# Second half's spectra read into the place of K's second spectrum, with four banks for the last transform and two middle row groups transformed ahead of the mixing

## The chip, the core and the metric

The kernel runs on one core of a Trainium2 chip. The metric is device time in microseconds, the median of several executions of one program. Engines are named as in the profile: PE (TensorE matmuls), PEld (its weight loads), DVE (VectorE), ACT (ScalarE), POOL (GpSimd), SP (SyncE, which here only issues DMAs).

## What is computed

A block of a model with two parts, on 2048 rows of 512 channels, in float32:

```python
h = _layernorm(x, axis=-1) * (1 + ca) + sa
x = x + ga * _A_ref(h, ...)      # long convolution by FFT: K from an SSM, Uf * Kf, inverse FFT
h = _layernorm(x, axis=-1) * (1 + cb) + sb
x = x + gb * _B_ref(h, B_w1, B_w2, B_w3, B_w4)
# _B_ref: gelu(layernorm(h) @ w1), four shifts along the rows, @ w2, + h;
#         then gelu(layernorm(.) @ w3) @ w4
```

## The kernel before, in words

The order of the instructions on every engine is written out by hand. It has four stages.

First the convolution kernel K is made and the input is normalised and transformed (until about 245 us of the trace). Then come 16 steps `(jh, kc)`, eight for each half `jh` of the channels: the spectra of the input and of K (tile `VK[jh]`, 32 KB in each partition) are made, multiplied, transformed back one level (`back`), and stored in DRAM as `ZT[jh]`.

The third stage is the last level of the inverse transform, with matmuls against the constant `FI`. `load_inv(jh, k)` reads one eighth of `ZT[jh]`, 512 KB, or 256 KB for half of it. The result is needed by row groups `g` (0 to 3) and halves `i`: 256 rows each, added to the tile `X2` (the trace calls it KX). A group 0 or 3 needs spectra 0, 3, 4 and 7; a group 1 or 2 needs spectra 1, 2, 5 and 6. `inv_half` makes the rows in a bank of PSUM and DVE adds them to X2; `inv_onto` first puts X2 into the bank with an identity matmul, lets the rows accumulate onto it, and ACT copies the sum back. The banks are `py` (pool `psy`, two of them) and `pm` (pool `psw`).

The fourth stage is the MLP part. It works on eight tiles `t` of 256 rows, in the order 7, 0, 1, 2, ...: statistics (`first_stats`), scale and shift (`mix_mod1`, `mix_mod2` on DVE), normalisation (`mix_norm` on ACT, `h<-h,nm,rs`), transposes on PE (`pT`), high and low parts (`parts_of`: ACT `nh`, then DVE `nl`), the product with w1 in two halves (`mix_half`: PE `pm`, 48 matmuls in pairs; ACT `go`), and a store to DRAM (`GD`). The channel part (`chan`, w3 and w4) follows tile by tile. Tiles 7 and 0 need row groups 3 and 0, tiles 1 and 2 come from rows of groups 0 and 1, tile 4 and later from group 2.

So the second half of the channels (`jh` = 1) must be read back right before the mixing starts. Its `ZT[1]` is complete only after the last `back`. Before the change, its eight spectra are read into six blocks `ld`, which also serve other loads: the first four take blocks that are free, the spectra 1 and 5 take the blocks of w2 (free when DVE has split w2), and 2 and 6 take the blocks of 3 and 7 (free when PE has transformed group 3 and group 0). All twelve reads stand on SP's queue, one behind the other. Meanwhile `keep(n)` issues n matmuls whose results are not used.

Rows of group 1 (`a10`, `a11`) are transformed between the two halves of tile 7's product, those of group 2 (`a20`, `a21`) behind the transposes of tiles 0 and 1.

Of the kernel before, what the change touches and what calls it, by code (L numbers as in the profile page):

```python
# [7 lines left out]
F32 = mybir.dt.float32  # L8
# [4 lines left out]
PSUM = bass.MemoryType.PSUM  # L13
# [96 lines left out]
def dram(t, off, ap):  # L110
    return bass.AP(tensor=t.tensor, offset=t.offset + off, ap=ap)


def body(ctx, tc, A):
# [6 lines left out]
    def act(out, in_, f=AF.Copy, scale=1.0, bias=0.0):  # L121
        return S.activation(out, in_, f, bias=bias, scale=scale)  # L122
# [105 lines left out]
    def mod_sum(n):  # L228
        k = MODS[n]
        m = psu.tile([128, 512], F32, name="pu")  # L230
        T.matmul(m, SP4, wmt.pop(n)[:, 0], start=True, stop=True)
        if k in (1, 4):
            return lambda: act(mods[k], m, AF.Identity, bias=1.0)
        return lambda: act(mods[k], m)
# [263 lines left out]
    side = {k: [] for k in range(40)}  # L498
    for k in range(8):
        w, i = ("w3", k) if k < 4 else ("w4", k - 4)  # L500
        n = A[w].shape[0] // 4
# [3 lines left out]
    for n in range(3, 6):  # L505
        k = 7 * n - 9
# [33 lines left out]
    with tc.manual_schedule():  # L540
# [13 lines left out]
        late = [lambda: later.append(mod_sum(2))]  # L554
# [36 lines left out]
        for f in later:  # L591
# [5 lines left out]
    a2 = ExitStack()  # L597
# [4 lines left out]
    VK = [v0x.enter_context(pool("v0", side="right")).tile([128, 64, 2, 64], F32, name="VK0"),  # L602
          c2.tile([128, 64, 2, 64], F32, name="VK1")]
# [6 lines left out]
    block = lambda: ldp.tile([128, 4, 256], F32, name="ld")  # L610
# [18 lines left out]
    vus, zis, zcs = {}, {}, {}  # L629
# [27 lines left out]
    def spectrum_k(jh, kc):  # L657
        p = [kbank([128, 2, 2, 128]) for gh in range(2)]
        for i in range(2):
            for ro in range(2):  # L660
                for ri in range(2):
                    for kk in range(2):
                        for gh in range(2):
                            k1 = kc * 4 + 2 * kk + i
                            rows = slice(gh * 64, gh * 64 + 64)
                            w = T2[k1 // 16][rows, k1 % 16]
                            if ri == gh:
                                w = w[:, ro * 64:ro * 64 + 64]
                            elif ro == ri:
                                w = w[:, gh * 64:gh * 64 + 64]  # L670
                            else:
                                w = T3[rows, k1]
                            T.matmul(p[gh][kk * 64:kk * 64 + 64, i, ro], w,  # L673
                                     VK[jh][rows, ri * 32 + k1].rearrange("p j g -> p (j g)"),
                                     start=(ri == 0), stop=(ri == 1), skip_group_check=True)
        return p
# [32 lines left out]

    def load_inv(jh, k, i=None, q=Y):  # L710
        if (jh, k) not in zis:
            zis[jh, k] = block() if jh or k in (1, 2, 5, 6) else zip_.tile([128, 4, 256], F32, name="zi")
        a, n = (0, 4) if i is None else (2 * i, 2)
        q.dma_start(zis[jh, k][:, a:a + n], dram(ZT[jh], (k * 4 + a) * 32768, [[256, 128], [32768, n], [1, 256]]))

# [3 lines left out]
    def inv_rows(p, jh, g, i, first):  # L719
        for e in range(2):  # L720
            b = g * 4 + i * 2 + e
            for bp, (c, sg) in enumerate(((31 - b, 1), (15 - b, 1), (b, 0), (16 + b, 0))):
                T.matmul(p[bp * 32:bp * 32 + 32, e], FI[:, c, sg], zis[jh, c // 4][:, c % 4],
                         start=first, stop=True, skip_group_check=True)

    def rows_of(jh, g, i):
        return X2[:, g * 4 + i * 2:g * 4 + i * 2 + 2, jh * 256:jh * 256 + 256]

    def inv_half(jh, g, i, pl, name):
        p = pl.tile([128, 2, 256], F32, name=name)  # L730
        inv_rows(p, jh, g, i, True)
        x = rows_of(jh, g, i)
        return lambda: V.tensor_add(x, p, x)

    def inv_onto(jh, g, i, pl, name):
        p = pl.tile([128, 2, 256], F32, name=name)
        x = rows_of(jh, g, i)
        T.matmul(p, ident, x, start=True, stop=False, skip_group_check=True)

        def rows():  # L740
            inv_rows(p, jh, g, i, False)
            return lambda: act(x, p)
        return rows
# [51 lines left out]
    def first_stat(b):  # L795
        if (b + 2) % 16 < 10:
            half_stat(b, 1)
            V.bn_aggr(mv1[:, b], st1[:, (b + 2) % 16])
        else:
            stats(mv1[:, b], X2[:, b])  # L800
        rstd(rs1[:, b:b + 1], mv1[:, b, 1:2])

    def first_stats(g):
        first_stat(2 * g)
        first_stat(2 * g + 1)
# [9 lines left out]
    def parts_of(ps):  # L815
        hi = [cm.tile([128, 2, 256], F32R, name=f"nh{j}") for j in range(2)]
        lo = [cm.tile([128, 2, 256], F32R, name=f"nl{j}") for j in range(2)]
        for j in range(2):
            act(hi[j], ps[j])
            V.tensor_sub(lo[j], ps[j], hi[j].bitcast(F32))  # L820
        return [hi[k // 2][:, k % 2] for k in range(4)], [lo[k // 2][:, k % 2] for k in range(4)]
# [3 lines left out]
    def mix_mod1(g):  # L825
        mh[g] = (cm.tile([128, 2, 512], F32, name="h2"), cm.tile([128, 2, 2], F32, name="mv"),
                 cm.tile([128, 2], F32, name="rs"), cm.tile([128, 2], F32, name="nm"))
        for i in range(2):
            mod1(mh[g][0][:, i], 2 * g + i)

    def mix_mod2(g, i, near=False):
        h, mv, r, nm = mh[g]
        mod2(h[:, i], 2 * g + i)
        stats(mv[:, i], h[:, i])
        if near:
            V.tensor_scalar(r[:, i:i + 1], mv[:, i, 1:2], 1e-5, None, op0=OP.add)
            V.tensor_scalar(nm[:, i:i + 1], mv[:, i, 0:1], -1.0, None, op0=OP.mult)
            P.tensor_tensor(r[:, i:i + 1], r[:, i:i + 1], pw[:, :1], op=OP.pow)
            P.tensor_tensor(nm[:, i:i + 1], nm[:, i:i + 1], r[:, i:i + 1], op=OP.mult)
            return  # L840
        rstd(r[:, i:i + 1], mv[:, i, 1:2])
        P.tensor_tensor(nm[:, i:i + 1], mv[:, i, 0:1], m_one[:, :1], op=OP.mult)
        P.tensor_tensor(nm[:, i:i + 1], nm[:, i:i + 1], r[:, i:i + 1], op=OP.mult)

    def mix_norm(g):
        h, mv, r, nm = mh[g]
        for i in range(2):
            act(h[:, i], h[:, i], AF.Identity, scale=r[:, i:i + 1], bias=nm[:, i:i + 1])
# [98 lines left out]
    def mix_half(t, hl, hf, between=None):  # L947
        p = mix_w(hl, hf, between)
        go = gop.tile([128, 2, 256], F32, name="go")
        act(go, p, AF.Gelu_apprx_tanh)  # L950
        mix_out(t, hf, go)
# [163 lines left out]
    with tc.manual_schedule():  # L1115
# [13 lines left out]
        for n, st in enumerate(steps):  # L1129
            p = spectrum_k(*st)  # L1130
            multiply(*st, us, p)
            if n == 7:
# [4 lines left out]
                zip_ = zix.enter_context(pool("zi", bufs=4, side="right", reuse_waits="tile"))  # L1137
# [12 lines left out]
            if n == 11:  # L1150
                for k in (0, 3, 4, 7):
                    load_inv(0, k)
            if n == 12:
                for k in (1, 2, 5, 6):
                    load_inv(0, k)
# [15 lines left out]
        tp = lambda name, bufs=1, **k: pool(name, bufs, reuse_waits="tile", **k)  # L1171
# [6 lines left out]
            act(W2h[:, i], w2r[i // 2][:, i % 2])  # L1178
        psT = ctx.enter_context(tp("psT", space=PSUM))
        psw = ctx.enter_context(tp("psw", 2, space=PSUM))  # L1180
        psy = a2.enter_context(tp("psy", 2, space=PSUM, side="right"))
        def keep(n):
            d = psT.tile([128, 2, 256], F32, name="pT0").rearrange("p a b -> p (a b)")
            for _ in range(n):
                T.matmul(d, W1h[:, 0, :128], W1h[:, 0], start=True, stop=True)
# [17 lines left out]
        for k in (1, 2):  # L1203
# [1 line left out]
            load_inv(1, k + 4)  # L1205
        onto = [inv_onto(1, g, i, pl, n) for g, i, pl, n in
                ((3, 1, psy, "py"), (0, 0, psy, "py"), (3, 0, psw, "pm"), (0, 1, psw, "pm"))]
        keep(8)
        for f in [f() for f in onto]:
            f()  # L1210
        first_stats(7)
        keep(14)
        mix_mod1(7)
        mix_mod2(7, 0, True)
        mix_mod2(7, 1, True)
        mix_norm(7)
        first_stats(0)
        mix_mod1(0)
        hl = parts_of(transposed(mh.pop(7)[0]))
        mix_mod2(0, 0, True)  # L1220
        mix_mod2(0, 1, True)
        mix_half(7, hl, 0)
        a10 = inv_half(1, 1, 0, psy, "py")
        a11 = inv_half(1, 1, 1, psy, "py")
        mix_norm(0)
        first_stats(1)
        a10()
        mix_half(7, hl, 1)
        mix_mod1(1)
        hl = parts_of(transposed(mh.pop(0)[0]))  # L1230
        mix_mod2(1, 0)
        mix_mod2(1, 1)
        a11()
        a20 = inv_half(1, 2, 0, psy, "py")
        mix_half(0, hl, 0)
        mix_norm(1)
        first_stats(2)
        mix_half(0, hl, 1)
        mix_mod1(2)
        hl = parts_of(transposed(mh.pop(1)[0]))  # L1240
        a21 = inv_half(1, 2, 1, psy, "py")
        mix_mod2(2, 0)
        a20()
        mix_mod2(2, 1)
# [33 lines left out]
        n = cm.tile([128, 2, 512], F32, name="h2")  # L1278
# [49 lines left out]
```

## Time and profile before

| what | value |
|---|---|
| median of 3 executions | 679.2 us (676.43 to 679.76) |
| the profiled execution: its own time | 677.66 us |
| its span in the trace | 675.9 us |
| mean granted TensorE clock | 0.997 |
| busy share of the span: PE, DVE, ACT, POOL | 94%, 73%, 50%, 17% |

The span runs from the first to the last instruction; the execution's own time has 1.76 us more around it. The profiled execution is 1.54 us below the median.

### The profile page before, as it was taken

The page shows a single profiled execution, that of the slowest core. Times are in us where ns is not written, and L with a number is a line of the kernel's source. Part 1 is how long each engine was busy: PE and PEld are TensorE (multiplying, and loading weights), DVE is VectorE, ACT ScalarE, POOL GpSimd, SP SyncE. Part 2 cuts the span into 40 slices and gives each one's busy share as a digit, 9 for nine tenths or more (in the row PEclk, how much of TensorE's full clock was granted, in tenths as well). Part 3 has the DMA queues.
Part 4 walks back from the last instruction along what each step waited for, and adds up shares of the span by engine and source line. Part 5 has one row for each costly group of instructions (what it writes and reads, how often), then busy time and mean ns, then how long its engine had stood idle before and what let it go on. Part 6 is the DMA issues. An engine that isn't in the chain of part 4 may idle for free.

```text
span 675.9 us, 16884 instructions
## 1 busy us (share of the span) xinstructions
PE 636.7 (94%) x7205; PEld 508.2 (75%) x7205; DVE 494.2 (73%) x797; ACT 335.8 (50%) x511; POOL 113.7 (17%) x220
## 2 busy tenths in 40 slices
PE   2899999999999998988999999999999999999996
PEld 1556555665568876645889899898998989898895
DVE  7889999999996897897889777454674445363622
ACT  5778998898884666624456334132141213122121
POOL 2102212112207133203643002010010000000000
PEclk9999999999999999998999999999999999999999
DMA  9602274642838999966386020110100201010001
GB/s 318 277 2 75 75 230 107 197 136 76 294 71 296 302 361 377 366 199 194 118 267 232 1 64 1 55 40 16 57 22 31 64 18 46 1 63 1 1 32 31
DMA packets 49923, 86.43 MB, mean 128 GB/s; under 512 B 4532, under 2 KB 38328, under 8 KB 47256
## 3 DMA queue, kind: packets, MB, share of 16 engines
q1 hardware_dynamic: 44904, 60.97, 28.3%
q0 software_dynamic: 4624, 23.86, 9.8%
q8 instruction: 56, 0.92, 0.6%
q10 hardware_dynamic: 320, 0.52, 0.3%
q14 instruction: 19, 0.16, 0.1%
HBM read 59.12 MB, written 32.90 MB: 136 GB/s over the span
## 4 chain that ended last, share of the span: by engine, by line
PE 72%; DMA 5%; DVE 5%; ACT 3%; issue 2%; POOL 1%; SPq 1%; ACTq 0%; DVEq 0%; POOLq 0%
PE xx L440 7%; PE pm L856 7%; PE pm L854 7%; PE pm L853 7%; PE pa L972 6%; PE pa L973 6%; PE pa L980 6%; PE pk L673 4%; PE kp L490 3%; DMA w4l<-Dw 2%; PE pz L695 2%; PE pk L643 2%; PE ph L911 2%; PE ph L910 2%; PE ph L913 2%
## 5 line engine op out<-in xcount | busy, mean ns | idle before, releaser
L122 ACT ACTIVATE gh<-pm 128x512 fp32r<-128x512 f32 (+1 forms) x48 | 26.9, 561 | 199.2 <-PE pm L856 199.2
L853 PE MATMUL pm<-nh,w3h 128*128 128x256 f32 (+1 forms) x352 | 85.9, 278 | 0.0
L854 PE MATMUL pm<-nh,w3l 128*128 128x256 f32 (+1 forms) x352 | 85.7, 279 | 0.1
L964 DVE TENSOR_TENSOR gl<-gf,gh 128x512 fp32r<-128x512 f32 (+1 forms) x48 | 30.9, 643 | 68.1 <-ACT gf L122 68.1
L972 PE MATMUL pa<-w4h,gh 128*128 128x512 f32 (+1 forms) x176 | 69.6, 395 | 0.0
L973 PE MATMUL pa<-w4l,gh 128*128 128x512 f32 (+1 forms) x176 | 68.9, 392 | 0.0
L854 PEld LDWEIGHTS pm<-nh,w3l 128*128 128x128 f32 (+1 forms) x352 | 65.2, 185 | 2.0 <-DVE w3l L767 0.3
L853 PEld LDWEIGHTS pm<-nh,w3h 128*128 128x128 f32 (+1 forms) x352 | 65.3, 186 | 1.4
L856 PE MATMUL pm<-nl,w3h 128*128 128x256 f32 (+1 forms) x352 | 54.9, 277 | 0.1
L774 POOL TENSOR_TENSOR rs<-mv,eps_t 128x1 f32<-128x1 f32 (+1 forms) x35 | 9.2, 264 | 267.3 <-DVE mv L780 251.5
L980 PE MATMUL pa<-w4h,gl 128*128 128x512 f32 (+1 forms) x176 | 48.0, 390 | 0.0
L441 PE MATMUL xx<-MG,ON 64*128 64x512 f32 x160 | 47.1, 390 | 0.0
L440 PE MATMUL xx<-MG,ON 64*128 64x512 f32 x160 | 47.1, 390 | 0.0
L856 PEld LDWEIGHTS pm<-nl,w3h 128*128 128x128 f32 (+1 forms) x352 | 46.6, 185 | 0.3 <-DVE nl L820 0.3
L916 DVE TENSOR_TENSOR h<-h,ph 128x512 f32<-128x512 f32 x16 | 11.0, 688 | 45.0 <-PE ph L913 45.0
L458 DVE SCALAR_TENSOR_TENSOR e<-tr,p 128x512 f32<-128x512 f32 x64 | 41.1, 684 | 1.7 <-ACT tr L122 1.4
L467 DVE TENSOR_TENSOR e<-tr,p 128x1024 f32<-128x1024 f32 x32 | 39.0, 1218 | 1.1 <-ACT tr L122 1.1
L490 PEld LDWEIGHTS kp<-e,e 128*32 128x32 f32 x2048 | 30.1, 110 | 12.7 <-issue 7.5
L468 DVE TENSOR_TENSOR e<-tr,m 128x1024 f32<-128x1024 f32 x32 | 39.0, 1218 | 0.0
L122 ACT ACTIVATE p<-xx 128x1024 f32<-128x1024 f32 (+1 forms) x40 | 37.5, 980 | 2.1 <-PE xx L258 0.6
L980 PEld LDWEIGHTS pa<-w4h,gl 128*128 128x128 f32 (+1 forms) x176 | 33.0, 188 | 7.1
L673 PE MATMUL pk<-VK,xu 64*64 64x128 f32 x768 | 35.9, 270 | 2.2 <-issue 2.2
(259 smaller groups left out, 1709.8 us busy)
## 6 DMA issues: line engine op xcount, KB each, us to landing
VU<-vs SPq DMA_DIRECT2D x64, 128.0 KB, 3.6
ld<-VU SPq DMA_DIRECT2D x16, 512.0 KB, 7.5
ZT<-z POOLq DMA_DIRECT2D x30, 256.0 KB, 6.3
Dw<-in_w POOLq DMA_DIRECT2D x8, 688.0 KB, 4.6
xu<-in_u SPq DMA_DIRECT2D x4, 1024.0 KB, 8.6
KX<-in_x POOLq DMA_DIRECT2D x4, 1024.0 KB, 9.0
ld<-ZT SPq DMA_DIRECT2D x8, 512.0 KB, 5.6
win<-GD SPq DMA_DIRECT2D x32, 128.0 KB, 2.5
```

The source lines that it names most:

```text
L122: return S.activation(out, in_, f, bias=bias, scale=scale)
L440: T.matmul(x[:, :512], la, ma, start=(i == 0), stop=(i == len(ops) - 1))
L441: T.matmul(x[:, 512:], lb, mb, start=(i == 0), stop=(i == len(ops) - 1))
L458: V.scalar_tensor_tensor(e0[:, 1, a], tr[:, 1, 0], 1.0 - 2.0 * a, mg[:, a], op0=OP.mult, op1=OP.mult)
L490: T.matmul(kp[32 * j:32 * j + 32, (k % 2) * 4 + g], e1[:, r, d], e0[:, r, :, d * 32:d * 32 + 32], start=(r == 0), stop=(r == 1), skip_grou ...
L673: T.matmul(p[gh][kk * 64:kk * 64 + 64, i, ro], w, VK[jh][rows, ri * 32 + k1].rearrange("p j g -> p (j g)"), start=(ri == 0), stop=(ri == 1 ...
L853: T.matmul(p, wh[:, k, c], hi[k], start=(k == 0), stop=False)
L854: T.matmul(p, wl[:, k, c], hi[k], start=False, stop=False)
L856: T.matmul(p, wh[:, k, c], lo[k], start=False, stop=(k == 3))
L972: T.matmul(acc[i], gh[:m, e, s], W4h[:m, f], start=(f == 0), stop=False)
L973: T.matmul(acc[i], gh[:m, e, s], W4l[:m, f], start=False, stop=False)
L980: T.matmul(acc[i], gl[:m, e, s], W4h[:m, f], start=False, stop=(f == 10))
```

## The change

The second half's eight spectra no longer take blocks `ld`: each has a place of 4 KB a partition in `VK[1]`, the tile that held K's second spectrum. `psy` has four banks in place of two. Both halves of group 1 are now made with `inv_onto` (their identity matmuls stand with the other four, their sums are copied by ACT), and both groups 1 and 2 are transformed ahead of tile 7's transposes. The first `keep(8)` is dropped and `keep(14)` becomes `keep(6)`.

```diff
     def load_inv(jh, k, i=None, q=Y):
         if (jh, k) not in zis:
-            zis[jh, k] = block() if jh or k in (1, 2, 5, 6) else zip_.tile([128, 4, 256], F32, name="zi")
+            if jh:
+                zis[jh, k] = VK[1].rearrange("p a b c -> p (a b c)")[:, k * 1024:k * 1024 + 1024].rearrange("p (n d) -> p n d", n=4)
+            else:
+                zis[jh, k] = block() if k in (1, 2, 5, 6) else zip_.tile([128, 4, 256], F32, name="zi")
...
-        psy = a2.enter_context(tp("psy", 2, space=PSUM, side="right"))
+        psy = a2.enter_context(tp("psy", 4, space=PSUM, side="right"))
...
-        keep(8)
+        late = [inv_onto(1, 1, i, psy, "py") for i in range(2)]
         for f in [f() for f in onto]:
             f()
         first_stats(7)
-        keep(14)
+        keep(6)
+        late = [f() for f in late]
+        a20 = inv_half(1, 2, 0, psy, "py")
+        a21 = inv_half(1, 2, 1, psy, "py")
         mix_mod1(7)
         mix_mod2(7, 0, True)
         mix_mod2(7, 1, True)
         mix_norm(7)
+        for f in late:
+            f()
         first_stats(0)
         mix_mod1(0)
         hl = parts_of(transposed(mh.pop(7)[0]))
         mix_mod2(0, 0, True)
         mix_mod2(0, 1, True)
         mix_half(7, hl, 0)
-        a10 = inv_half(1, 1, 0, psy, "py")
-        a11 = inv_half(1, 1, 1, psy, "py")
         mix_norm(0)
         first_stats(1)
-        a10()
         mix_half(7, hl, 1)
         mix_mod1(1)
         hl = parts_of(transposed(mh.pop(0)[0]))
         mix_mod2(1, 0)
         mix_mod2(1, 1)
-        a11()
-        a20 = inv_half(1, 2, 0, psy, "py")
         mix_half(0, hl, 0)
...
         hl = parts_of(transposed(mh.pop(1)[0]))
-        a21 = inv_half(1, 2, 1, psy, "py")
         mix_mod2(2, 0)
         a20()
         mix_mod2(2, 1)
```

PE, from the last rows of the first half's transform to tile 7's product, before (a matmul of this listing appears as two in the trace; `FI` is the transform's constant, `w1h` alone marks `keep`):

```order
L723 MATMUL py<-ld,FI 32x256 x16
L738 MATMUL py<-KX,ident 128x512 x2
L738 MATMUL pm<-KX,ident 128x512 x2
L1185 MATMUL pT_4604<-w1h 128x512 x8
L723 MATMUL py<-ld,FI 32x256 x16
L723 MATMUL pm<-ld,FI 32x256 x16
L1185 MATMUL pT_4657<-w1h 128x512 x14
L812 MATMUL pT_4710<-ident,h_4672 128x128 x4
L812 MATMUL pT_4711<-ident,h_4672 128x128 x4
L853 MATMUL pm<-nh_4720,w1h 128x256
```

The same place of PE after the change (lines of the changed file are three higher):

```order
L726 MATMUL py<-ld,FI 32x256 x16
L741 MATMUL py<-KX,ident 128x512 x2
L741 MATMUL pm<-KX,ident 128x512 x2
L741 MATMUL py<-KX,ident 128x512 x2
L726 MATMUL py<-VK_3051,FI 32x256 x16
L726 MATMUL pm<-VK_3051,FI 32x256 x16
L1188 MATMUL pT_4644<-w1h 128x512 x6
L726 MATMUL py<-VK_3051,FI 32x256 x32
L815 MATMUL pT_4725<-ident,h_4685 128x128 x4
L815 MATMUL pT_4726<-ident,h_4685 128x128 x4
L856 MATMUL pm<-nh_4735,w1h 128x256
```

Thirty-two matmuls of groups 1 and 2 have come in ahead of tile 7's transposes; they stood in three places of the mixing (16, 8 and 8), where nothing stands now.

ACT, from the same stage, before (`KX<-py` and `KX<-pm` are the copies of `inv_onto`, `h` the normalisation, `nh` the high parts of the transposed tile):

```order
L122 ACTIVATE KX<-py 128x2x256 x2
L122 ACTIVATE KX<-pm 128x2x256 x2
L122 ACTIVATE h_4672<-h_4672,nm,rs 128x512 x2
L122 ACTIVATE nh_4720<-pT_4710 128x512
L122 ACTIVATE nh_4721<-pT_4711 128x512
```

And after:

```order
L122 ACTIVATE KX<-py 128x2x256 x2
L122 ACTIVATE KX<-pm 128x2x256 x2
L122 ACTIVATE h_4685<-h_4685,nm,rs 128x512 x2
L122 ACTIVATE KX<-py 128x2x256 x2
L122 ACTIVATE nh_4735<-pT_4725 128x512
L122 ACTIVATE nh_4736<-pT_4726 128x512
```

Two copies (group 1's sums) now stand between the normalisation of tile 7 and its high parts; in their place two adds `KX<-py` are gone from DVE. SP's and POOL's queues issue the same transfers in the same order, SP's twelve reads into another tile.

## Rows read from the trace of the kernel before

**Rows 1.** The page: the span, and each engine's busy time.
```profile
span 675.9 us, 16884 instructions
PE 636.7 (94%) x7205; PEld 508.2 (75%) x7205; DVE 494.2 (73%) x797; ACT 335.8 (50%) x511; POOL 113.7 (17%) x220
```

**Rows 2.** Windows by stage: busy us of each engine, granted clock, DMA share, GB/s.
```profile
300.00:306.00 6.00, 2.26 (x13) 1.47 (x15) 4.10 (x7) 0.00 (x0) 0.00 (x0) 1.00 0.89 259
...
318.00:326.00 8.00, 8.00 (x84) 6.84 (x82) 6.87 (x18) 3.76 (x6) 4.71 (x12) 1.00 0.20 68
...
350.00:360.00 10.00, 10.00 (x65) 8.97 (x64) 8.63 (x16) 4.51 (x9) 2.76 (x5) 1.00 0.99 349
```

**Rows 3.** Timeline of SP's queue: start, us; reads of the second half's spectra.
```profile
299.41 13.14 SPq L714 DMA_DIRECT2D ld<-ZT  x12
...
311.64 0.91 SPq L714 DMA_DIRECT2D ld<-ZT  x2
```

**Rows 4.** Windows of one microsecond while the spectra arrive; columns as in Rows 2.
```profile
306.00:307.00 1.00, 1.00 (x24) 0.61 (x20) 0.00 (x0) 0.06 (x1) 0.00 (x0) 0.96 1.02 330
307.00:308.00 1.00, 1.00 (x16) 0.33 (x8) 0.42 (x1) 0.54 (x1) 0.00 (x0) 0.50 0.98 324
308.00:309.00 1.00, 0.42 (x4) 0.00 (x0) 0.71 (x4) 0.53 (x1) 0.53 (x2) 0.50 1.07 366
309.00:310.00 1.00, 0.89 (x12) 0.43 (x16) 0.85 (x2) 0.06 (x1) 0.92 (x3) 0.50 1.05 346
310.00:311.00 1.00, 1.00 (x20) 0.53 (x16) 1.00 (x2) 0.17 (x1) 0.35 (x1) 0.83 0.64 201
311.00:312.00 1.00, 1.00 (x14) 0.53 (x7) 0.96 (x2) 0.68 (x2) 0.00 (x0) 1.00 0.15 36
```

**Rows 5.** Timeline of PE and PEld up to tile 7's transposes; in brackets the idle time before.
```profile
289.95 1.93 PE L723 MATMUL pk<-zi,FI 128*32 128x256 f32 x32
...
291.70 1.91 PE L723 MATMUL pk<-ld,FI 128*32 128x256 f32 x32
...
299.66 2.41 PE L1185 MATMUL pT<-w1h 128*128 128x512 f32 x8
...
305.81 2.61 PE L723 MATMUL py<-ld,FI 128*32 128x256 f32 x32 [3.74 <-DMA ld<-ZT]
...
309.11 0.20 PEld L723 LDWEIGHTS pm<-ld,FI 128*32 128x32 f32 x8 [1.57 <-DMA ld<-ZT]
...
311.55 3.49 PE L1185 MATMUL pT<-w1h 128*128 128x512 f32 x14
...
316.05 0.87 PE L812 MATMUL pT<-ident,h 128*128 128x128 f32 x6 [0.45 <-ACT h L122]
```

**Rows 6.** Timeline of DVE: the low parts of tiles 7, 0 and 1.
```profile
317.16 1.29 DVE L820 TENSOR_TENSOR nl<-pT,nh 128x512 fp32r<-128x512 f32 x2 [0.45 <-ACT nh L122]
...
326.50 1.29 DVE L820 TENSOR_TENSOR nl<-pT,nh 128x512 fp32r<-128x512 f32 x2 [1.36 <-ACT nh L122]
...
334.34 1.29 DVE L820 TENSOR_TENSOR nl<-pT,nh 128x512 fp32r<-128x512 f32 x2 [0.29 <-ACT nh L122]
```

**Rows 7.** Timeline of ACT in the same stretch.
```profile
316.53 1.09 ACT L122 ACTIVATE nh<-pT 128x512 fp32r<-128x512 f32 x2 [0.53 <-PE pT L812]
...
323.02 0.82 ACT L122 ACTIVATE h<-h,nm,rs 128x512 f32<-128x512 f32 x1 [0.54 <-POOL nm L839]
325.38 0.60 ACT L122 ACTIVATE go<-pm 128x512 f32<-128x512 f32 x1 [1.54 <-PE pm L856]
325.87 1.08 ACT L122 ACTIVATE nh<-pT 128x512 fp32r<-128x512 f32 x2
...
332.37 0.82 ACT L122 ACTIVATE h<-h,nm,rs 128x512 f32<-128x512 f32 x1 [0.39 <-POOL nm L843]
```

**Rows 8.** Timeline of PE: the rows of groups 1 and 2 inside the mixing.
```profile
320.36 1.93 PE L723 MATMUL py<-ld,FI 128*32 128x256 f32 x32
...
326.15 1.07 PE L723 MATMUL py<-ld,FI 128*32 128x256 f32 x16
...
334.04 1.07 PE L723 MATMUL py<-ld,FI 128*32 128x256 f32 x16
```

## Prediction

> **What bounds the kernel now.** I read the page first, then windows over the stage that the diff touches, then the timelines of SP, PE, ACT and DVE there. PE is busy for 94% of the span [rows 1], but the stage from the last `back` to tile 7's product is not a PE stage. In 300 to 306 us PE works 2.26 of 6.00 us while the DMA engines are busy to 0.89 [rows 2]: it is waiting for the spectra that have just been stored. SP issues the first read at 299.41 us and the last two only at 311.64 us [rows 3], because these two wait for blocks that PE still reads. PE waits 3.74 us until 305.81 us for the first four reads and its weight loads 1.57 us until 309.11 us for the next four; a `keep` of 14 matmuls fills the time until the normalised tile 7 is there, and the last transposes start at 316.05 us, released by ACT's `h` [rows 5]. From there PE is full: 8.00 of 8.00 us in 318 to 326 us, 10.00 of 10.00 us in 350 to 360 us, where the DMA engines are also at 0.99 with w3 and w4 [rows 2]. So a delay or a gain at tile 7's transposes is passed on to the end unless the chain behind it has slack.
>
> That chain is best read on DVE. `nl` of tiles 7, 0 and 1 start at 317.16, 326.50 and 334.34 us [rows 6], which is 9.34 and 7.84 us apart. Each `nl` waits for ACT's `nh`, and leads by the next tile's scale, statistics and normalisation to the next `nh`.
>
> **What the change does, part by part.**
>
> *The reads.* All twelve go on SP without a wait for a block; the first eight are where they were. They carry 8 x 256 KB = 2.10 MB, and the last four 4 x 512 KB = 2.10 MB more. Today the ninth and tenth run on behind the eighth, then the DMA engines fall to 0.64 and 0.15 busy in 310 to 312 us, for the eleventh and twelfth are not issued yet [rows 4]. After the change nothing interrupts the stream. The eighth lands at 309.11 us, when the weight loads that wait for it start [rows 5]. The mean rate of 306 to 310 us is (330 + 324 + 366 + 346) / 4 = 341 GB/s [rows 4], so 2.10 MB take 6.1 us and the twelfth lands at about 315.2 us. Bounds: the ten reads are nearly through by 310.6 us (0.64 of that microsecond), and the other 1.05 MB at 341 GB/s take 3.1 us: 313.7 us. At the 259 GB/s of 300 to 306 us [rows 2] they take 8.1 us: 317.2 us. I take 315.2 us, since a landing that PE waited for is the thing to extrapolate from.
>
> *The 32 matmuls in the new place (64 in the trace).* A row group 1 or 2 needs all of spectra 1, 2, 5 and 6, so the first of these matmuls waits for the last read, and tile 7's transposes stand behind them on PE. Sixty-four such matmuls ran from 289.95 to 291.70 + 1.91 = 293.61 us, 3.66 us [rows 5]. They end at 315.2 + 3.7 = 318.9 us. From the transposes to `nl` it takes 317.16 - 316.05 = 1.1 us today, with two of the eight transposes already done [rows 5, 6]; with all eight I take 1.2 us. `nl` of tile 7 then starts at 320.1 us in place of 317.16 us: **3.0 us late**, between 1.4 us (read landed at 313.7) and 4.9 us (317.2). The scale and normalisation of tile 7 are done by 316 us as now and simply wait, and so does `nh` behind them on ACT. ACT's two new copies need the first half of the block, done at about 317 us, and lie in ACT's wait; their cost is nothing under that cover, and two copies, 0.5 to 0.6 us each, if the cover were gone (the same shape as `go` [rows 7]).
>
> *What leaves the mixing.* Between the halves of tile 7 there are 32 trace matmuls of 1.93 us, and 16 of 1.07 us behind each of the two next transposes [rows 8]: 4.1 us of PE. The question is what they hold up. In tile 7's interval, ACT's second `h` of tile 0 ends at 323.02 + 0.82 = 323.84 us, 6.68 us after `nl`, but `go` and `nh` follow only at 325.38 and 325.87 us, because PE was late with the half and the transposes [rows 6, 7]. In the next interval the second `h` ends at 332.37 + 0.82 = 333.19 us, 6.69 us after `nl`, and the next `nl` comes 1.15 us behind it [rows 6, 7]: there the path is DVE, POOL and ACT, and not PE. Without the 1.93 us, tile 7's interval becomes like that one: 9.34 - 7.84 = **1.5 us gained**. The other two blocks of 1.07 us lie exactly where PE waits for `nh`, and gain nothing: bound 1.07 us each if PE alone set the pace. For the first block the ends are 0 and 1.93 us; I take 1.5 us, since the second interval shows what remains.
>
> *The rest.* Two adds of DVE are gone, but they stood behind the statistics that lead to the next normalisation: no gain. Four banks: the identity matmuls no longer wait for DVE's adds, but the spectra come later than all of them. `keep(8)`, 2.41 us from 299.66 us [rows 5], is replaced by two identity matmuls; PE idles a little longer before 305.81 us, and what follows there is paced by the reads. `keep(6)` is 6/14 of 3.49 us = 1.5 us, from 311.55 to about 313.0 us [rows 5], which leaves PE idle for 2.2 us before the block. SP's later issues (stores of GD, w3, w4) depend on `go` and move with the chain, so the DMA stage of 350 us moves with PE and doesn't absorb it.
>
> *Sum.* 3.0 - 1.5 = **+1.5 us**. On the profiled execution's own 677.66 us that is 679.2 us; since that execution was 1.54 us below the median of the runs shown, the median becomes about 680.7 us. I call it no measurable change: 0.5% is 3.4 us, about what a measurement of this kernel can tell from no change.
>
> **The rivals.**
>
> *1. PE alone paces the mixing.* PE's 8.00 of 8.00 us [rows 2] speak for it. Then all 4.1 us come off: 3.0 - 4.1 = -1.1 us, and -2.7 us if the reads land at 313.7 us: 676.5 to 678.1 us. Against it speaks that `nl` follows `h` by the same path in the interval in which PE had less work [rows 6, 7]. Still inside 0.5%. Chance 0.20. "Perfetto Trace Analysis" in the Trainium skill, under Matmul Optimizations, says to use all eight banks of PSUM so that work overlaps; that is this rival's side, while the rows here show the banks idle for want of data.
>
> *2. PE's clock falls while it waits for the last reads (slower).* The row shows it today: after 3.74 us idle PE starts the 32 matmuls of 305.81 us, the granted clock goes from 0.96 to 0.50 (the 1.2 GHz level) in 307 to 310 us, and they take 2.61 us in place of 1.93 us [rows 4, 5, 8]. In the new place the idle time before the 64 matmuls is 2.2 us; it reaches 3.7 us if the last read lands at 316.8 us or later. At half clock the block costs 3.7 us more: with the landing at 315.2 us +5.2 us, 684.4 us, and 1.6 us above that with the late landing: slower by 0.8 to 1.0%. Against it: 2.2 us is shorter than what preceded the fall in the row. Chance 0.13. "TensorE: Matmul & The Clock Gate" in the Trainium skill, under HAM oscillation, describes just this, a PE that waits for DMA and then runs its short burst at half clock; by that page the change trades `keep` matmuls for the risk.
>
> *3. The new tile is waited for as a whole.* If the first matmuls of group 3 had to wait for all twelve reads into `VK`, everything would start at 315.2 us in place of 305.81 us: 9.4 - 1.5 = +7.9 us, 687.1 us. The order lists the first group's matmuls and group 1's as separate blocks, and the reads are the same twelve pieces in their own slices. Chance 0.03.
>
> The forecast itself has 0.60; 0.04 is left for what I don't see.
>
> **How the numbers follow.** The forecast's own bounds are 1.4 - 1.5 = -0.1 us and 4.9 - 1.5 = +3.4 us: 679.1 to 682.6 us. Rival 1 reaches down to 676.5 us, and the three runs shown differ by 3.3 us among themselves. I take 676.9 to 683.6 us, which leaves out most of rivals 2 and 3. Slower by over 0.5%: rivals 2 and 3 and the upper edge of the forecast, 0.19. Faster by over 0.5% needs 675.8 us, below every case: 0.07. Within 0.5%: 0.74.
>
> **What would show it.** In the new trace: twelve reads issued by about 306 us and DMA at 0.9 or more until 314 to 315 us; PE idle from about 313 us, then 64 matmuls on `VK` from 315 us, and tile 7's `nl` at about 320 us; then `nl` to `nl` about 7.8 us twice, with PE idle before each `pm`. The forecast is wrong if the block starts before 313.5 us, if the clock is 0.50 in it, or if the second interval of `nl` falls clearly below 7.8 us. The last would mean that PE did set the pace, and the two blocks that I price at nothing were worth up to 1.07 us each.

## The result, and the profile after

The changed kernel takes 681.34 us (median of 22 runs) and the kernel before 678.65 us (22 runs on the same chip): a ratio of 1.0036, 95% interval 1.0021 to 1.0051. So it is slower, beyond the noise, by 0.36%; that is less than the 0.5% that was set as the bound for a change, though the interval reaches just past it. The forecast was 680.7 us. The ratios here and below, with their intervals, come from the fast executions alone and are not quotients of the medians beside them, which also count three slow executions (912.18 us of the kernel before beside e1, e2, e3 and e5, 724.59 us of e2 and 1247.74 us of e3).

The page of the changed kernel, against [rows 1]: PE is as busy as before, and the span is 3.8 us longer in this execution (its own time is 681.49 us).
```profile
span 679.7 us, 16856 instructions
PE 636.0 (94%) x7193; PEld 508.1 (75%) x7193; DVE 493.1 (73%) x795; ACT 337.1 (50%) x513; POOL 113.8 (17%) x220
```
Not all of the 3.8 us is the change's: the stage begins 1.30 us later in this trace (SP's first read at 300.71 us against 299.41 us [rows 3]), and what runs before it is the same program. I therefore count from SP's first read in every trace below. From there to the end it is 379.0 us after and 376.5 us before: 2.5 us longer.

SP's queue in the changed kernel, against [rows 3]: one group of twelve, and nothing at 311.64 us any more.
```profile
300.71 7.63 SPq L717 DMA_DIRECT2D VK<-ZT  x12
```
Windows of the changed kernel while the spectra arrive, columns as in Rows 2 (us, busy us of PE, PEld, DVE, ACT and POOL, granted clock, DMA share, GB/s). They answer to [rows 4].
```profile
306.00:310.00 4.00, 3.08 (x32) 1.46 (x36) 0.43 (x1) 0.60 (x1) 0.00 (x0) 0.50 1.04 325
310.00:312.00 2.00, 2.00 (x24) 0.90 (x20) 1.58 (x5) 0.60 (x1) 1.47 (x4) 0.50 1.08 357
...
314.00:315.00 1.00, 0.86 (x4) 0.38 (x2) 0.96 (x4) 0.00 (x0) 0.55 (x1) 1.00 1.03 330
315.00:316.00 1.00, 0.00 (x0) 0.00 (x0) 0.93 (x3) 0.19 (x1) 0.69 (x2) 1.00 0.28 90
316.00:317.00 1.00, 0.00 (x0) 0.00 (x0) 0.93 (x6) 0.62 (x1) 0.61 (x2) 1.00 0.05 15
```
The hole of 310 to 312 us is gone, the DMA engines are full until 315 us, and then there is a tail: 90 and 15 GB/s for two microseconds, in which PE does nothing at all. The clock column shows PE at half clock (1.2 GHz) from 306 to 312 us, about twice as long as before.

PE's timeline in the changed kernel, against [rows 5]; in brackets the idle time before, and what ended it.
```profile
306.92 3.64 PE L726 MATMUL py<-VK,FI 128*32 128x256 f32 x32 [3.78 <-DMA VK<-ZT]
310.34 2.93 PE L726 MATMUL pm<-VK,FI 128*32 128x256 f32 x32
313.20 1.65 PE L1188 MATMUL pT<-w1h 128*128 128x512 f32 x6
317.31 3.66 PE L726 MATMUL py<-VK,FI 128*32 128x256 f32 x64 [2.45 <-DMA VK<-ZT]
320.90 1.09 PE L815 MATMUL pT<-ident,h 128*128 128x128 f32 x8
```
The 64 matmuls start as soon as the last read has landed, 16.60 us after the first read was issued, and tile 7's transposes stand behind them.

DVE's timeline in the changed kernel: `nl` of tiles 7, 0 and 1, against [rows 6], and one row between them that the reading below needs.
```profile
322.22 1.29 DVE L823 TENSOR_TENSOR nl<-pT,nh 128x512 fp32r<-128x512 f32 x2 [3.54 <-ACT nh L122]
...
330.06 1.29 DVE L823 TENSOR_TENSOR nl<-pT,nh 128x512 fp32r<-128x512 f32 x2 [0.28 <-ACT nh L122]
331.26 1.01 DVE L789 SCALAR_TENSOR_TENSOR h<-h,rs,modg 128x512 f32<-128x512 f32 x1
...
335.80 1.36 DVE L786 SCALAR_TENSOR_TENSOR h<-KX,mv,modg 128x512 f32<-128x512 f32 x2
338.56 1.29 DVE L823 TENSOR_TENSOR nl<-pT,nh 128x512 fp32r<-128x512 f32 x2 [1.39 <-ACT nh L122]
```
Tile 7's `nl` comes 21.51 us after the first read, in place of 17.75 us: 3.76 us late. Tile 7's interval is 330.06 - 322.22 = 7.84 us in place of 9.34 us. The next one, which the forecast left as it was, grew from 7.84 to 338.56 - 330.06 = 8.50 us. POOL's timeline in the changed kernel shows what ran beside the two other rows of DVE:
```profile
331.21 0.52 POOL L885 COPY win<-go 128x384 f32<-128x384 f32 x1
331.65 0.77 POOL L886 COPY win<-go 128x124 f32<-128x124 f32 x1
...
335.96 0.59 POOL L846 TENSOR_TENSOR nm<-nm,rs 128x1 f32<-128x1 f32 x1
```
The copies are those that make the shifted edge of tile 7's second half. Beside them DVE's L789, 0.74 us elsewhere in the same trace, takes 1.01 us; and beside DVE's L786, POOL's `nm`, 0.19 us elsewhere, takes 0.59 us. Both stand on the chain to the next `nl`.

From the fourth `nl` on next to nothing differs: from that of tile 2 to the end of the span it is 331.5 us after and 331.7 us before.

**What the theories are.** Mine is that of the prediction: the wait for the last read, with the 64 matmuls ahead of tile 7's transposes, is the loss; the 1.93 us of PE taken out of tile 7's interval are the gain; the two blocks of 1.07 us are worth nothing. The rivals are that PE alone paces the mixing, that the clock is the loss, and that the place of the reads costs something by itself. The table gives every run's median, its ratio to the kernel before (whose median was 678.74 us beside e1, e2, e3 and e5, 678.75 us beside e4, e6 and e7, and 679.24 us beside e8 to e10), and from its one trace the time from the first read to tile 7's `nl` and the next three intervals of `nl`.

| kernel | us | ratio (95%) | nl(7) | 7 to 0 | 0 to 1 | 1 to 2 |
|---|---|---|---|---|---|---|
| before | 678.65 | 1 | 17.75 | 9.34 | 7.84 | 9.83 |
| changed | 681.34 | 1.0036 (1.0021–1.0051) | 21.51 | 7.84 | 8.50 | 9.65 |
| e1 | 678.31 | 0.9995 (0.9979–1.0012) | 17.72 | 9.33 | 7.84 | 9.81 |
| e2 | 680.36 | 1.0025 (1.0008–1.0042) | 20.68 | 7.84 | 8.50 | 9.64 |
| e3 | 678.64 | 0.9992 (0.9977–1.0008) | 18.91 | 7.83 | 8.50 | 9.65 |
| e4 | 678.25 | 1.0008 (0.9988–1.0029) | 18.53 | 9.34 | 7.83 | 9.82 |
| e5 | 677.74 | 0.9990 (0.9972–1.0007) | 17.73 | 7.84 | 8.49 | 9.65 |
| e6 | 676.85 | 0.9980 (0.9964–0.9997) | 18.68 | 7.90 | 7.91 | 9.82 |
| e7 | 679.94 | 1.0029 (1.0010–1.0047) | 22.58 | 7.84 | 8.23 | 9.56 |
| e8 | 676.70 | 0.9967 (0.9950–0.9984) | 17.28 | 7.90 | 7.92 | 9.82 |
| e9 | 678.08 | 0.9994 (0.9979–1.0010) | 17.79 | 10.70 | 7.83 | 9.82 |
| e10 | 680.40 | 1.0024 (1.0001–1.0046) | 23.24 | 7.83 | 8.10 | 9.23 |

### The profile page after: what moved, and what is told of

Read it like the earlier page. It is cut to its first block, busy times and chain, and to the rows that moved or that the text cites. A ratio compares the mean times of both kernels' runs of the same rounds, so it can differ in the third digit from the quotient of the medians.

```text
span 679.7 us, 16856 instructions
## 1 busy us (share of the span) xinstructions
PE 636.0 (94%) x7193; PEld 508.1 (75%) x7193; DVE 493.1 (73%) x795; ACT 337.1 (50%) x513; POOL 113.8 (17%) x220
## 4 chain that ended last, share of the span: by engine, by line
PE 74%; DVE 6%; issue 3%; DMA 3%; ACT 3%; POOL 0%; SPq 0%; ACTq 0%; DVEq 0%; POOLq 0%
PE xx L440 7%; PE pm L859 7%; PE pm L857 7%; PE pm L856 7%; PE pa L975 6%; PE pa L976 6%; PE pa L983 6%; PE pk L673 4%; PE kp L490 3%; PE pz L695 2%; DMA VK<-ZT 2%; PE ph L913 2%; PE ph L914 2%; PE pk L619 2%; PE ph L916 2%
```

## The experiments

**e1_reads_only: the reads alone.** The kernel before with the first hunk of the change (the spectra of the second half in `VK[1]`) and nothing else.

> The kernel before with one edit: the second half's spectra are read into K's second spectrum; order of PE, banks and keep matmuls as before. My theory (the loss comes from the 64 matmuls that wait for the last read ahead of tile 7's transposes): here nothing waits for the last four reads, which land some 2 us earlier than before and are used 4 us later, so 0 us against the kernel before, within 0.7 us; nl of tile 7 17.7 us after SP's first read, as before. Rival (the new place of the reads itself costs, by waits for the whole tile or by DMA traffic): slower by 1 us or more, and PE's first spectra matmul more than 6.4 us after SP's first read.

Nothing moves: `nl` of tile 7 17.72 us after the first read, the intervals those of before, ratio 0.9995. The reads' new place costs nothing, and since the first row groups still start at 305.58 us, 6.2 us after the first read, they don't wait for all twelve. That removes the third rival.

**e2_keeps_back: PE kept busy.** The changed kernel with the two keeps of the kernel before:
```
+        keep(8)
         for f in [f() for f in onto]:
             f()
         first_stats(7)
-        keep(6)
+        keep(14)
```


> The changed kernel with both keep stretches as in the kernel before (8 and 14 matmuls in place of none and 6). My theory: PE is warmer and less idle, but the block still waits for the last read, so the time is that of the changed kernel, about 2.5 us over the kernel before, within 0.8 us of it. Rival (the loss is the clock: in the changed kernel the granted clock is 0.50 for 6.8 us, before it was for 3.4 us): the second half-clock window goes and the loss shrinks by 1 us or more.

Most of the loss stays: by the medians it is 1.6 us in place of 2.7 us. That is the 1 us less which the rival asked for, but the two intervals of the ratio overlap. In PE's timeline of e2 the 64 matmuls now start 0.12 us behind the longer keep, 15.77 us after the first read (299.12 us):
```profile
305.68 2.68 PE L726 MATMUL py<-VK,FI 128*32 128x256 f32 x32 [2.29 <-DMA VK<-ZT]
...
311.26 3.51 PE L1188 MATMUL pT<-w1h 128*128 128x512 f32 x14
314.89 3.66 PE L726 MATMUL py<-VK,FI 128*32 128x256 f32 x64
```
They are at full clock (3.66 us, as in the changed kernel), and tile 7's `nl` is still 2.9 us late. From the block's start to `nl` it is 4.91 us in both kernels; the 0.83 us by which `nl` is earlier here are the block's earlier start. So in this execution the last read had landed at 15.77 us or earlier. A lower clock is not what the change loses by: the long stretch at half clock is gone in this trace (0.50 from 307 to 310 us only, as in [rows 4]), the median of the mean granted clock over all executions is 0.997 in e2 against 0.994 in the kernel before beside it, and e2 is still slower.

**e3_early_spectra: nothing to wait for.** The changed kernel, with row groups 1 and 2 of the second half made from spectra 0, 3, 4 and 7, which land first; these rows of the output are other numbers, the work is the same.
```
+        near = {1: 0, 2: 3, 5: 4, 6: 7} if jh else {}
...
-                T.matmul(p[bp * 32:bp * 32 + 32, e], FI[:, c, sg], zis[jh, c // 4][:, c % 4],
+                T.matmul(p[bp * 32:bp * 32 + 32, e], FI[:, c, sg], zis[jh, near.get(c // 4, c // 4)][:, c % 4],
```


> The changed kernel, but the rows of groups 1 and 2 of the second half are made from spectra 0, 3, 4 and 7, which have landed by then, in place of 1, 2, 5 and 6 (all twelve reads are still issued): the wait for the last read is taken away, the output's second half of these rows is another. My theory: the block runs straight behind the keep matmuls and ends at about the time the normalised tile 7 is there, nl of tile 7 comes 18 to 19 us after SP's first read (21.5 in the changed kernel, 17.7 before), and the time is 2.5 to 3.5 us below the changed kernel's, 0 to 1 us below the kernel before. Rival (the block's PE time or the copies on ACT cost, not the wait): less than 1 us below the changed kernel.

PE's timeline of e3, and DVE's:
```profile
313.95 3.66 PE L727 MATMUL py<-VK,FI 128*32 128x256 f32 x64
```
```profile
319.55 1.29 DVE L824 TENSOR_TENSOR nl<-pT,nh 128x512 fp32r<-128x512 f32 x2 [0.78 <-ACT nh L122]
```
The block starts behind the keep of 6, at 313.95 us, 13.31 us after the first read (300.64 us) in place of 16.60 us, and `nl` is 1.16 us late in place of 3.76 us. Of the 1.16 us, 0.87 are half clock in the first block (ACT's first copy follows the block's start by 2.00 us in place of 1.13), and 0.3 are ACT's two new copies, which start at 317.97 us, behind the normalisation, and now hold up `nh`. The median is 678.64 us, 2.7 us under the changed kernel's. This is the cleanest of the runs: the same instructions, without the wait for the last read, and the loss is gone.

**e4_no_group2 and e5_no_group1: what the blocks in the mixing were worth.** Both are the kernel before with work left out, so that rows of the output differ: e4 leaves out the matmuls of row group 2 (its adds stay and read group 1's banks), e5 the matmuls and adds of row group 1. First e4's edit, cut to what leaves PE, then e5's:
```
-        a20 = inv_half(1, 2, 0, psy, "py")
...
-        a21 = inv_half(1, 2, 1, psy, "py")
```
```
-        a10 = inv_half(1, 1, 0, psy, "py")
-        a11 = inv_half(1, 1, 1, psy, "py")
...
-        a10()
...
-        a11()
```


> The kernel before, without row group 2's 32 matmuls in the trace (two blocks of about 1.07 us behind the transposes of tiles 0 and 1); the two adds of DVE stay and add row group 1's result once more, so group 2's rows of the second half come out different. Theory (these two blocks fill PE's wait for nh and cost nothing): the intervals from nl to nl stay at 9.34, 7.84 and 9.8 us, within 0.2 us each, and the time within 0.5 us of the kernel before. Rival (PE alone sets the pace): the second and third interval shorten by 1.07 us each, 2.1 us off the time, ratio 0.997.

> The kernel before without the second half's rows of group 1: 32 trace matmuls between tile 7's halves and two adds of DVE are left out, so the output lacks them. It prices what the change takes out of the mixing. My theory: the interval of nl from tile 7 to tile 0 falls from 9.3 to 7.8 us and is then paced by DVE, POOL and ACT; 1.5 us faster than before, within 0.6. Rival (PE paces): the whole 1.9 us and the later PE work too, 2 us or more faster, with PE never idle before tile 0's transposes.

DVE's timeline of e4, whose two blocks of 1.07 us are gone:
```profile
318.69 1.29 DVE L820 TENSOR_TENSOR nl<-pT,nh 128x512 fp32r<-128x512 f32 x2 [1.54 <-ACT nh L122]
...
328.03 1.29 DVE L820 TENSOR_TENSOR nl<-pT,nh 128x512 fp32r<-128x512 f32 x2 [1.36 <-ACT nh L122]
...
335.86 1.29 DVE L820 TENSOR_TENSOR nl<-pT,nh 128x512 fp32r<-128x512 f32 x2 [0.29 <-ACT nh L122]
```
9.34 and 7.83 us: to a hundredth what they were. (Tile 7's `nl` is 0.8 us late in this trace because the half clock lasted over the second block, 3.64 us in place of 2.51 us, and into the keep, 3.99 us in place of 3.49 us [rows 5], and the transposes stand behind them; this delay is not group 2's.) Without group 1, in e5, tile 7's interval is 7.84 us, and PE waits there for ACT ahead of the rest of the transposes:
```profile
323.42 0.88 PE L812 MATMUL pT<-ident,h 128*128 128x128 f32 x6 [0.40 <-ACT h L122]
```
PE alone doesn't pace the mixing; that rival falls, and in the traces both prices of the prediction (1.5 us and nothing) are right. The times fit, but can't show it: e5's median is 1.0 us below the kernel before's, and the interval of its ratio takes in 1. But e5 shows the interval of 8.49 us as well, though its reads, banks and keeps are those of before. DVE's timeline of e5:
```profile
316.69 1.29 DVE L820 TENSOR_TENSOR nl<-pT,nh 128x512 fp32r<-128x512 f32 x2 [0.45 <-ACT nh L122]
...
324.53 1.29 DVE L820 TENSOR_TENSOR nl<-pT,nh 128x512 fp32r<-128x512 f32 x2 [0.29 <-ACT nh L122]
...
333.02 1.29 DVE L820 TENSOR_TENSOR nl<-pT,nh 128x512 fp32r<-128x512 f32 x2 [1.39 <-ACT nh L122]
```
The longer second interval belongs to group 1's leaving the mixing.

**e7_no_copies and e10_one_add_back: where 0.66 us went.** e7 is the changed kernel without POOL's copies for the edge tiles (the edges are stored unshifted, so these rows of the output differ). e10 is the changed kernel with one add of group 2 moved forward to where an add of group 1 had been; it computes all. In `mix_out`, e7 drops the copies and memsets and stores `go` in place of `pd`:
```
-            P.tensor_copy(pv[:, :, 0:96], gv[:, :, 32:128])
-            P.tensor_copy(pv[:, :, 96:127], gv[:, :, 1:32])
...
-            P.tensor_copy(pv[:, :, 32:128], gv[:, :, 0:96])
-            P.tensor_copy(pv[:, :, 1:32], gv[:, :, 96:127])
```
e10's edit:
```
         mix_mod2(1, 1)
+        a20()
...
         mix_mod2(2, 0)
-        a20()
```


> The changed kernel without POOL's eight copies and four memsets for the edge tiles 7 and 0 (each half's edge is stored from go unshifted, so the rows at the image's edge come out different; the number and size of the stores stay). Theory (the second interval grew from 7.84 to 8.50 us because these copies now run beside DVE's step on the path, which takes 1.01 us in place of 0.74, and hold up POOL's statistics): the second interval falls back to 7.7 to 7.9 us, the time 0.6 us below the changed kernel or a little more, ratio to the kernel before about 1.003. Rival (the second interval is longer for another reason, such as PE's transposes or the shorter first interval itself): it stays at 8.4 to 8.6 us, ratio 1.0036 as the changed kernel.

The interval is 8.23 us: neither. DVE's timeline of e7:
```profile
332.13 1.29 DVE L823 TENSOR_TENSOR nl<-pT,nh 128x512 fp32r<-128x512 f32 x2 [0.45 <-ACT nh L122]
...
337.61 1.36 DVE L786 SCALAR_TENSOR_TENSOR h<-KX,mv,modg 128x512 f32<-128x512 f32 x2
340.36 1.29 DVE L823 TENSOR_TENSOR nl<-pT,nh 128x512 fp32r<-128x512 f32 x2 [1.39 <-ACT nh L122]
```
0.27 us are the copies' (DVE's L789 takes 0.74 us again), and 0.39 us stay. POOL's timeline of e7 shows them:
```profile
337.48 0.21 POOL L845 TENSOR_TENSOR nm<-mv,m_one 128x1 f32<-128x1 f32 x1
337.77 0.58 POOL L846 TENSOR_TENSOR nm<-nm,rs 128x1 f32<-128x1 f32 x1
```
DVE's L786 of tile 2 starts at 337.61 us there, 5.48 us after `nl`. In the kernel before the same step (L783 there) starts at 332.58 us, 6.08 us after its `nl` of 326.50 us [rows 6], because an add of group 1 stands ahead of it:
```profile
330.89 0.66 DVE L733 TENSOR_TENSOR KX<-py,KX 128x512 f32<-128x512 f32 x1
...
332.58 1.47 DVE L783 SCALAR_TENSOR_TENSOR h<-KX,mv,modg 128x512 f32<-128x512 f32 x2
```
That made the second half of the theory, which e10 tries.

> The whole computation. The changed kernel with the first add of row group 2 put where the second add of row group 1 stood in the kernel before, ahead of the statistics and scaling (L786) that DVE does for tile 2. Theory (of the 0.66 us by which the second interval grew, the copies on POOL cost 0.27 us, as e7 showed, and 0.39 us come from DVE's scaling starting earlier by the add that was taken out, so that POOL's nm runs beside it and takes 0.59 us in place of 0.19): nm takes 0.19 us again and the second interval is 8.1 us in place of 8.50; the time 0.3 us below the changed kernel, too little for the ratio. Rival (the place of the add has nothing to do with it): the interval stays at 8.5 us, or grows by the add's 0.66 us.

With the add in its old place the step takes 0.19 us again, and the interval is 8.10 us, as expected. POOL's row of `nm` in e10's timeline:
```profile
335.09 0.19 POOL L846 TENSOR_TENSOR nm<-nm,rs 128x1 f32<-128x1 f32 x1
```
And DVE's, the `nl` of tiles 0 and 1:
```profile
329.18 1.29 DVE L823 TENSOR_TENSOR nl<-pT,nh 128x512 fp32r<-128x512 f32 x2 [0.28 <-ACT nh L122]
...
337.28 1.29 DVE L823 TENSOR_TENSOR nl<-pT,nh 128x512 fp32r<-128x512 f32 x2 [0.29 <-ACT nh L122]
```
So 0.27 + 0.39 = 0.66 us, both from POOL and DVE standing in each other's way. (This is read from one trace each; the times of e7 and e10 can't tell, for their intervals overlap the changed kernel's.) "SBUF — State Buffer" in the Trainium skill, under Who interferes with whom, says that a DVE instruction with two inputs in SBUF and a GpSimd instruction that reads SBUF exclude one another, and that the one that issues first keeps the other waiting. The changed kernel's rows agree: L789 and L786 have two such inputs; L789 starts after POOL's copy (331.26 and 331.21 us) and takes 1.01 us for 0.74, and POOL's `nm` starts after L786 (335.96 and 335.80 us) and takes 0.59 us for 0.19.

e7 and e10 show something more, in PE's timeline of the block. In e7:
```profile
317.69 5.35 PE L726 MATMUL py<-VK,FI 128*32 128x256 f32 x64 [2.74 <-DMA VK<-ZT]
```
And in e10:
```profile
314.75 5.35 PE L726 MATMUL py<-VK,FI 128*32 128x256 f32 x64 [2.97 <-DMA VK<-ZT]
```
The 64 matmuls take 5.35 us in place of 3.66 us. Windows of e7 show why (columns as above, the granted clock third from the end):
```profile
318.00:319.00 1.00, 1.00 (x20) 0.53 (x16) 0.80 (x2) 0.15 (x2) 0.92 (x3) 0.74 0.00 0
319.00:320.00 1.00, 1.00 (x16) 0.49 (x12) 0.00 (x0) 0.54 (x1) 0.48 (x1) 0.50 0.00 0
```
The granted clock is 0.50 in the block. This is the prediction's second rival, seen in two of the three traces that have this wait at its full length. Its price is 1.7 us, not the 3.7 us of the prediction, because the clock was back before the block ended. With it, tile 7's `nl` is 4.8 us (e7) and 5.5 us (e10) late. "TensorE: Matmul & The Clock Gate" in the Trainium skill, under HAM oscillation, tells of this: PE waits for DMA and then runs its short burst at half clock. These two traces agree: PE waits 2.74 and 2.97 us, and the burst takes 5.35 us in place of 3.66 us.

**e6_in_the_waits: the matmuls behind the transposes.** The whole computation: the kernel before with the reads into `VK[1]` and four banks, and the blocks put where PE waits for `nh`. Its edit for tile 7; the second half of group 1 goes behind tile 0's transposes in the same way, and group 2 behind tile 1's.
```
-        hl = parts_of(transposed(mh.pop(7)[0]))
+        ps = transposed(mh.pop(7)[0])
+        a10 = inv_half(1, 1, 0, psy, "py")
+        hl = parts_of(ps)
```


> The whole computation. The kernel before with all twelve reads into VK and four banks, and the matmuls of row groups 1 and 2 put behind the transposes of the tiles: group 1's first half behind those of tile 7, its second half behind those of tile 0, group 2 behind those of tile 1; both keeps as before. Theory (the wait for the last read was the change's loss, the shorter first interval its gain): nl of tile 7 17.7 us after the first read as in the kernel before, the first interval 7.84 us in place of 9.34, the second 7.84 to 8.5 as in the changed kernel, the third 9.6 to 9.9; in sum 0.8 to 1.5 us below the kernel before, ratio 0.998 to 0.999. Rival (1.93 us of PE must be paid wherever they stand): the first and second interval get 1 us longer where the halves now stand, and the sum is nothing, ratio 1.000.

676.85 us, ratio 0.9980 with an interval that ends below 1. PE's rows of e6:
```profile
306.74 3.49 PE L726 MATMUL py<-VK,FI 128*32 128x256 f32 x32 [4.12 <-DMA VK<-ZT]
...
318.47 1.07 PE L726 MATMUL py<-VK,FI 128*32 128x256 f32 x16
319.47 0.39 PE L856 MATMUL pm<-nh,w1h 128*128 128x256 f32 x1
...
326.31 1.07 PE L726 MATMUL py<-VK,FI 128*32 128x256 f32 x16
```
And DVE's:
```profile
318.77 1.29 DVE L823 TENSOR_TENSOR nl<-pT,nh 128x512 fp32r<-128x512 f32 x2 [0.46 <-ACT nh L122]
...
326.67 1.28 DVE L823 TENSOR_TENSOR nl<-pT,nh 128x512 fp32r<-128x512 f32 x2
327.87 0.82 DVE L789 SCALAR_TENSOR_TENSOR h<-h,rs,modg 128x512 f32<-128x512 f32 x1
...
334.58 1.29 DVE L823 TENSOR_TENSOR nl<-pT,nh 128x512 fp32r<-128x512 f32 x2 [0.29 <-ACT nh L122]
```
The halves of group 1 follow the transposes without idle time. They outlast the wait for `nh`: tile 7's product starts 0.70 us after `nl` (319.47 us), in the kernel before 0.02 us after it. But the intervals are 7.90 and 7.91 us, so PE had that much to spare: the 1.44 us of tile 7's interval are kept. The second interval doesn't grow, for the adds stand ahead of L786 again, and POOL's copies hold L789 by only 0.08 us (0.82 us for 0.74). In this one trace `nl` of tile 7 is 0.93 us late: 0.25 us because the first block starts later after the first read (6.65 us for 6.40), and 0.70 us because the clock was at half over nearly the whole block (3.49 us, against 2.61 us in [rows 5]). What four banks do by themselves was not run.

**e8_no_gap and e9_before_no_gap: PE's wait for the first reads filled.** e8 is e6, and e9 the kernel before, each with `keep(20)` in place of `keep(8)`.

> The whole computation. e6_in_the_waits with a keep of 20 matmuls in place of 8 ahead of the first row groups' matmuls: at 0.30 us each (8 took 2.41 us) they fill PE's 3.74 us wait for the first four reads, which in every trace so far is followed by a fall of the granted clock to 0.50. Theory (this half clock lies on the path, since tile 7's statistics wait for the first of these blocks): the clock stays at 1.00 there, the first 32 matmuls take 1.93 us in place of 2.61 to 3.49, nl of tile 7 starts 16.9 to 17.2 us after the first read in place of 17.72 (kernel before) or 18.68 (e6), and the time is 0.7 to 1.5 us below e6: ratio to the kernel before 0.996 to 0.997. Rival (the statistics wait for something else, or the keep itself delays the block): nl of tile 7 stays at 17.7 us or later and the ratio at 0.998.

> The whole computation. The kernel before with the keep of 20 in place of 8 and nothing else. Theory: as in e8, the first block takes 1.93 us, nl of tile 7 17.0 us after the first read in place of 17.75, the intervals behind it unchanged (9.34, 7.84, 9.83), the time 0.7 us or a little more below the kernel before, ratio 0.999. Rival: no change of nl, ratio 1.000.

In e8's trace the first block is at full clock, as expected:
```profile
307.74 1.93 PE L726 MATMUL py<-VK,FI 128*32 128x256 f32 x32 [0.63 <-DMA VK<-ZT]
```
Its 676.70 us (ratio 0.9967) are the lowest of all. `nl` of tile 7 comes 17.28 us after the first read, 0.47 us earlier than in the kernel before, but that is the landing: the block starts 5.92 us after the first read in place of 6.40 us. And e9 falls to its rival: the first block takes 1.93 us there too, and `nl` of tile 7 stays at 17.79 us after the first read. ACT's first copy tells why: it needs only the first half of the block. In e9's timeline of ACT it starts 1.13 us after the block (307.37 us):
```profile
308.50 0.60 ACT L122 ACTIVATE KX<-py 128x512 f32<-128x512 f32 x1 [7.59 <-PE py L723]
```
From this copy to `nl` of tile 7 it is 10.20 us in e9, 10.22 us in e8 and 10.20 us in e6, and in the kernel before it is 10.22 us with the copy also 1.13 us behind the block's start (305.81 us [rows 5]): there the clock fell only after the first half was done. In e6 it fell almost at once, and the copy came 1.83 us behind the start. So the half clock in this block cost nothing in the kernel before and 0.7 us in e6, by when it fell (and in e4 0.8 us by another way, through the keep). And a busy PE ahead of it didn't hold the clock for good in e9: it fell later, in tile 7's product, whose interval is 10.70 us there. Windows of e9:
```profile
318.00:319.00 1.00, 0.75 (x6) 0.52 (x5) 0.55 (x2) 0.92 (x2) 0.85 (x2) 0.86 0.00 0
319.00:320.00 1.00, 1.00 (x6) 1.00 (x7) 1.00 (x3) 0.98 (x2) 0.00 (x0) 0.50 0.00 0
```
This trace is e9's slowest execution of twelve (680.52 us). Over all twelve the median of the mean granted clock is 0.9975, against 0.994 in the kernel before beside them: the filler did raise the clock, without a gain in time that the interval could tell from none.

That e8 gains over e6 is not shown: their intervals overlap. That both are faster than the kernel before is, and e8's interval, 0.9950 to 0.9984, is also wholly below the changed kernel's.

## Why the prediction was right, and where its terms were off

*The reads: right in kind, 0.2 to 0.8 us short.* The last landing was put at 315.2 us, 15.8 us after the first read. Where PE waited for it, it came 16.60 us (changed kernel), 15.98 us (e7) and 16.64 us (e10) after it, inside the bounds of 14.3 to 17.8 us; in e2 it had landed by 15.77 us, where the forecast put it. The mean rate carried to the last byte leaves out the tail, which the windows show at 90 and 15 GB/s behind 315 us.

*The block and the path behind it: exact.* 3.7 + 1.2 = 4.9 us were forecast, and it is 322.22 - 317.31 = 4.91 us at full clock. ACT's two new copies cost nothing, as said: `nh` waits for the transposes in any case. (Without that cover, in e3, they cost 0.3 us, not the 1.0 to 1.2 us that the prediction gave them.)

*Tile 7's `nl`: mis-sized.* Forecast 3.0 us late, measured 3.76 us. The difference of 0.8 us is the landing's. e3 shows that the wait is the cause.

*Tile 7's interval: exact.* 1.5 us shorter forecast; 9.34 to 7.84 us in the changed kernel, and within 0.01 us of that in e2, e3, e5, e7 and e10.

*The other two blocks: right.* Worth nothing, by e4.

*"Two adds of DVE are gone ... no gain": the step that failed.* No gain was right, but I didn't ask what starts earlier when they go. The second interval grew by 0.66 us, which e7 and e10 split into the copies beside L789 (0.27 us) and L786 beside `nm` (0.39 us).

*The sum.* In the trace 3.76 - 1.50 + 0.66 = 2.9 us; the third interval gives 0.2 us back and the rest of the program another 0.2, which leaves the 2.5 us between the two spans from the first read. The medians differ by 2.7 us, forecast 1.5 us. That the forecast median was closer, at 680.7 against 681.34 us, is luck: the kernel before was also 0.5 us faster in these runs than in the three that the sum was made against.

*The rivals.* PE as the pace is refuted (e4, e5), and so is the wait for the whole tile (e1). The half clock is real, where the prediction gave it 0.13: it isn't in the block in the changed kernel's own trace, but it is in e7 and e10. The prediction counted on it from 3.7 us of idle time on. That was wrong, for it came behind 2.74 and 2.97 us, and in e2's first block behind 2.29 us, while behind the changed kernel's 2.45 us it did not come; so was the price, which is 1.7 us and not 3.7 us. How often it falls into the block when the changed kernel runs can't be told from three traces.

## What to carry to other kernels

Work that waits for the last transfer doesn't belong ahead of the step that a chain waits for, even when it fills idle time there. Put it behind that step, where the engine waits for the chain anyway: against the kernel before, the same blocks cost 2.7 us in the one place (the changed kernel) and gained 1.9 us in the other (e6), by the medians. When an operation leaves an engine, ask what starts earlier in its stead, and what runs on the neighbouring engine at that time. And estimate a landing that something waits for from the last piece, with its tail, not from the mean rate of the stream.

## What the runs showed of the hardware that I had not expected

Removing one add of 0.66 us from DVE made the chain 0.39 us longer, through a step on POOL with one element per partition that went from 0.19 to 0.59 us.

Twenty matmuls in a wait of 3.7 us kept the clock at 1.00 through the wait and the block behind it, in e8 and e9. In e9 the clock then fell to 0.50 at about 318.7 us, after four waits of 0.57 to 1.11 us between blocks of matmuls; in e8, with waits of 0.45 to 1.16 us, it did not fall there. What made the difference stays open.
